# Attention and two feed-forward layers on one core: values with tokens on partitions, the square on another engine, and a new order for the first pass

## The chip, the cores and the metric

The kernel runs on one core of a Trainium2 chip. The metric is the device time of one execution in microseconds (us). Five engines work side by side, each through its own queue of instructions in order: TensorE (PE; its weight loads are listed as PEld), VectorE (DVE), ScalarE (ACT), GpSimd (POOL) and SyncE (SP), which in this kernel does little but issue DMAs.

## What is computed

```python
# attention inside chunks of 64 tokens; q, k, v are (4, 8, 576, 64): batch, heads, tokens, head size
scores = q_c @ k_c.T / 8
attn = softmax(scores)               # maximum taken off; the sum gets 1e-9 added
x = (attn @ v_c) as (2304 tokens, 512)
# layer 1, w_in (512, 2048), w_out (2048, 512)
r = max(x @ w_in, 0);  g = s * (r * r) + b;  x = g @ w_out
# layer 2, the same sizes with weights of its own
h = x @ w_in2;  g = h * tanh(softplus(h));  out = g @ w_out2
```

The weights arrive as 64-bit floats. The kernel reads them as pairs of 32-bit words and decodes each piece into a high and a low part; x and g are split in the same way, and each product is made of three matmuls (high by high, low by high, high by low).

## The kernel before

**Tiles, blocks, chunks.** The 2304 tokens are 18 tiles of 128. Tiles are joined into five blocks of 512, 256, 512, 512 and 512 tokens (`sizes`). The hidden size 2048 is cut into 16 chunks of 128 (d_ff chunks), and four chunks make a group, so each layer has four groups. For a group, each block is multiplied by its four chunks, and the sum of the four is added into `ysum`. The last 7 of 8 groups come from plain loops at the end of the kernel. Attention and the first group of layer 1, the first pass, come from an order written out by hand.

**The order table.** `START` is a string of pieces. `pieces` turns each into instructions, and every engine runs its own in the order of the string. A number is the tile, the weight piece or the step; `@4` names a PSUM bank, and the digit after a dot a buffer. SP has `dk`, `dq`, `dv` (load a tile's keys, queries, values, 256 KB each) and `W` (load a weight piece of 512 KB: 0 to 7 are the first group's, 8 to 15 the second's). PE has `K`, `Q`, `T` (four transposes each of keys, queries, probabilities), `S` (scores), `X` (attention output), `I` and `J` (the two halves of a step's first matmul, `mm_in`), `O` and `P` (the halves of its second, `mm_out`), and `w` followed by a number (that many matmuls on zeros). ACT has the copies out of PSUM `k`, `q`, `t`, the exponential `e`, the high half `x` of a tile's output, the decoding steps `a` and `h`, and `r` (ReLU), `v` (add b) and `g` (high half) of a step. DVE has `m` (row maximum and subtraction), `n` (row sum), `z` (division), `y` (low half), the decoding steps `c`, `d` and `l`, `u` (square times s) and `o` (low half). `E` moves a sum of a block to `ysum`, by turns on ACT and DVE.

A step of a 512-token block is 12 matmuls by the first weights and 12 by the second. A half, `I`, `J`, `O` or `P`, is 6 of them. Before, step i stands for block i // 4 and chunk i % 4.

**Attention of a tile.** Keys and queries are loaded with tokens on partitions, and `K` and `Q` transpose them. `k_out` writes the transposed keys into a block-diagonal buffer `kbd` (two copies of 64 partitions; zeroed by POOL at the start; three of them), so `s_pe` takes 8 matmuls of 128 rows by 64 columns over 128 moving columns. The values are loaded with pairs of heads on partitions, by four DMAs a tile (`load_v`), tile 0's from ACT's queue. `x_pe` takes 16 matmuls of 64 by 64 over 64 columns.

**Buffers that order the loads.** Tiles 0 to 3 keep their keys, queries and values in the room of weight pieces 8 to 15. Later tiles share two buffers for keys, two for queries and three for values, so such a load waits until the `K`, `Q` or `X` that read its buffer is done, and what stands behind it on SP waits too. The sums of a block hold the four PSUM banks `acc0` to `acc3` from its first `O` to its `E`; attention pieces with `@0` to `@3` use the same banks.

Of the kernel before, what the change touches and what calls it, by code (L numbers as in the profile page):

```python
# [9 lines left out]
F32 = mybir.dt.float32  # L10
# [43 lines left out]
def chunk_attention_moe_moe_kernel(  # L54
# [28 lines left out]
    sizes = [512, 256, 512, 512, 512]  # L83
# [120 lines left out]
    def sb_at(i, tag):  # L204

        if i >= NS:
            if tag == "pt":
                return at[i]["e"].rearrange("p h s -> p (h s)")
            return atp.tile([P, DM], F32, tag=tag, bufs=AT_BUFS[tag], name=tag)
        if (i, tag) not in early:  # L210
            if tag in ("e", "pt"):
                whole = sb.tile([P, KD, TB], F32, tag="xhi3" if tag == "e" else "xlo3", name=tag)
                for n in range(NS):
                    early[n, tag] = whole[:, n]
            else:
                both = ("q", "k") if tag in ("q", "k") else ("v", "qt")
                whole = sb.tile([P, 2, DM], F32, tag="w%d_%d" % (tag in ("v", "qt"), NSLOT - 1 - i), name=tag)
                for n, x in enumerate(both):
                    early[i, x] = whole[:, n]
        return early[i, tag]  # L220

    def load_qk(i, which):
        t = sb_at(i, which).rearrange("p (h d) -> p h d", h=H)
        for o, n, bb, ss in runs(i * P, P):
            nc.sync.dma_start(
                out=t[o:o + n],
                in_=(k if which == "k" else q)[bb, :, ss:ss + n, :].rearrange("h s d -> s h d"),
            )
        at.setdefault(i, {})[which] = t

    def load_v(i, eng=nc.sync):
        vn = sb_at(i, "v").rearrange("p (a c d) -> p a c d", a=KD, c=2)
        at.setdefault(i, {})["v"] = vn
        for o, n, bb, ss in runs(i * P, P):
            c0, cn = o // CH, n // CH
            for j in range(2):
                for c in range(cn):
                    eng.dma_start(
                        out=vn[j * CH:(j + 1) * CH, :, c0 + c, :],
                        in_=v[bb, j::2, ss + c * CH:ss + (c + 1) * CH, :].rearrange("a s d -> s a d"),  # L240
                    )
# [7 lines left out]
    def k_pe(i, b):  # L249
        at[i]["kp"] = transposes(b, at[i]["k"].rearrange("p h d -> p (h d)"))  # L250

    def k_out(i, n):
        at[i]["kb"] = kb = kbd[n]
        kp = at[i].pop("kp").rearrange("p a (c s) -> p a c s", c=2)
        for j in range(2):
            sl = slice(j * CH, (j + 1) * CH)
            nc.scalar.copy(out=kb[sl, :, :, sl], in_=kp[sl])  # L257
# [8 lines left out]
    def s_pe(i, b):  # L266
        t = at[i]
        t["sp"] = ps_at(b, [P, H, CH])
        for a in range(KD):
            for c in range(2):  # L270
                sl = slice(c * CH, (c + 1) * CH)
                nc.tensor.matmul(  # L272
                    out=t["sp"][sl, 2 * a:2 * a + 2, :].rearrange("p j s -> p (j s)"),
                    lhsT=t["qt"][:, a, sl],
                    rhs=t["kb"][:, a, c, :],
                )
# [29 lines left out]
    def p_out(i):  # L306
        at[i]["pt"] = sb_at(i, "pt").rearrange("p (a s) -> p a s", a=KD)
        nc.scalar.copy(out=at[i]["pt"], in_=at[i].pop("pp"))

    def x_pe(i, b):  # L310
        t = at[i]
        t["xp"] = ps_at(b, [P, KD, P])
        for a in range(KD):
            for c in range(2):
                for j in range(2):
                    r = slice(j * CH, (j + 1) * CH)
                    s = slice(c * CH, (c + 1) * CH)
                    nc.tensor.matmul(out=t["xp"][r, a, s], lhsT=t["v"][r, a, c, :], rhs=t["pt"][r, a, s])  # L318
# [66 lines left out]
    def mm_out(l, f, g, acc, n, h):  # L385

        w = wt[l, f, 1]
        last = f % FG == FG - 1
# [3 lines left out]
        for p, m in order[h * len(order) // 2:(h + 1) * len(order) // 2]:  # L392
# [6 lines left out]
                start=(f % FG == 0 and p == 0), stop=(last and p == 2),  # L399
# [43 lines left out]

    def pieces(name, i, m, bank):


        b, f = divmod(i, FG)
        n = sizes[b] if b < NB else 0
        if name in ("dk", "dq"):
            load_qk(i, name[1])  # L450
        elif name == "dv":
            load_v(i, nc.sync if i else nc.scalar)
# [5 lines left out]
        elif name == "k":  # L458
            k_out(i, m)
        elif name in "qmenztxy":  # L460
            dict(q=q_out, m=s_max, e=s_exp, n=s_sum, z=s_norm, t=p_out, x=x_hi, y=x_lo)[name](i)
# [13 lines left out]
        elif name == "u":  # L475
            ew_u(ff[i]["r"])
        elif name == "v":
            ew_v(ff[i]["r"])
        elif name == "g":
            ff[i]["g"] = ew_g(ff[i]["r"], n)  # L480
        elif name == "o":
            ff[i]["o"] = ew_o(ff[i]["r"], ff[i]["g"], n)
        elif name in "OP":
            if name == "O" and f == 0:
                first_acc[b] = new_accs(1, b)
            mm_out(1, f, (ff[i]["g"], ff[i]["o"]), first_acc[b], n, "OP".index(name))
        elif name == "E":
            first_sum(i, m, first_acc[i][m], nc.vector.tensor_copy if m % 2 else nc.scalar.copy)
        else:
            raise ValueError(name)  # L490

    with tc.manual_schedule():
# [5 lines left out]
        room = sb.tile([P, 2, KD, 2, P], F32, tag="ysum3", name="kbd12")  # L498
        kbd = [atp.tile([P, KD, 2, P], F32, name="kbd"), room[:, 0], room[:, 1]]
        for kb in kbd:  # L500
            nc.gpsimd.memset(kb, 0.0)
# [8 lines left out]
    def do_out():  # L510
# [3 lines left out]
        for h in range(2):  # L514
            mm_out(l, f, g, accs[l, b], sizes[b], h)
# [55 lines left out]
```

## Time and profile before

| | before |
|---|---|
| median of 3 runs | 889.46 us (888.0 to 890.33) |
| the profiled execution, its own time | 889.39 us |
| its span, first to last instruction | 887.6 us |
| PE busy | 874.8 us, 99% of the span |
| DVE, ACT busy | 477.7 us (54%), 370.9 us (42%) |
| DMA | 53.22 MB, mean 60 GB/s |

The span leaves 1.8 us of the execution's own time outside. A busy share is the share of the span in which the profile shows an instruction of that engine. Matmuls overlap, so the time from one start to the next is what one costs, and not the duration of its row; PE can be listed as busy while it runs slower than it could. The zero matmuls `w` count as busy.

### The profile page before, as it was taken

Reading aid. Unit: us, or ns where it says so; the run is one execution under the profiler, and the core shown is the slowest. Engines: PE = TensorE matmul, PEld = TensorE weight load, DVE = VectorE, ACT = ScalarE, POOL = GpSimd, SP = SyncE. Lnnn points to the kernel's source line nnn. Section 1 sums busy time; section 2 is a strip of 40 time slices with the busy share of each in tenths; the row PEclk is TensorE's granted clock in tenths of the full one; section 3 lists DMA queues with packets and bytes.
Section 4 is the critical chain, followed back from the end, with each engine's and each line's share of the span. In section 5 each row is a group of like instructions: output and inputs, shape, how many; then the busy total and the mean of one; then the engine's idle time right before and its main releaser. Section 6 shows DMA issues by size and latency. Waiting matters only on the chain.

```text
span 887.6 us, 12275 instructions
## 1 busy us (share of the span) xinstructions
PE 874.8 (99%) x4976; PEld 737.9 (83%) x4976; DVE 477.7 (54%) x852; ACT 370.9 (42%) x645; POOL 30.0 (3%) x29
## 2 busy tenths in 40 slices
PE   8989999999999999999999999999999999999997
PEld 7978888888888898888888888888888888888886
DVE  4878875459736943488348922473227722222122
ACT  5667665446534543345445432332223322222221
POOL 1000000000000000002122200000000000000000
PEclk9999999999999999999999999999999999999999
DMA  8996131040004200140004100230003100001012
GB/s 217 220 244 179 44 85 36 21 170 1 1 0 122 69 1 1 48 142 2 1 1 143 48 0 1 61 129 1 0 24 121 46 1 1 0 1 48 24 48 95
DMA packets 81528, 53.22 MB, mean 60 GB/s; under 512 B 58688, under 2 KB 75072, under 8 KB 81472
## 3 DMA queue, kind: packets, MB, share of 16 engines
q1 hardware_dynamic: 80384, 52.18, 20.4%
q8 instruction: 39, 0.64, 0.3%
q10 hardware_dynamic: 1088, 0.26, 0.1%
q14 instruction: 17, 0.14, 0.0%
HBM read 47.71 MB, written 4.72 MB: 59 GB/s over the span
## 4 chain that ended last, share of the span: by engine, by line
PE 97%; ACT 1%; DMA 1%; DVE 0%; issue 0%; DVEq 0%; ACTq 0%
PE hp L344 45%; PE acc L395 45%; PE warm L466 2%; DMA k<-in_k_dram 1%; PE pa L272 1%; ACT kbd L257 1%; PE pa L246 1%; PE pa L318 0%; DVE ysum L416 0%; ACT e L290 0%; ACT v L264 0%; PE pt__383 L272 0%; PE pt__195 L272 0%; PE pt__101 L246 0%; PE pt__2009 L318 0%
## 5 line engine op out<-in xcount | busy, mean ns | idle before, releaser
L344 PE MATMUL hp<-xhi,w 128*128 128x512 f32 (+1 forms) x1280 | 368.6, 369 | 0.3 <-ACT r L354 0.3
L344 PEld LDWEIGHTS hp<-xhi,w 128*128 128x128 f32 x1280 | 232.2, 188 | 41.9 <-issue 0.9
L344 PE MATMUL hp<-xlo,w 128*128 128x512 f32 (+1 forms) x640 | 235.5, 368 | 0.0
L374 DVE TENSOR_TENSOR glo<-r,ghi 128x512 fp32r<-128x512 f32 (+1 forms) x160 | 104.9, 655 | 208.5 <-ACT ghi L369 208.1
L395 PE MATMUL acc<-ghi,w 128*128 128x512 f32 (+1 forms) x640 | 162.8, 372 | 0.0
L395 PE MATMUL acc<-w,ghi 128*128 128x512 f32 x576 | 159.5, 390 | 0.0
L356 ACT ACTIVATE r<-hp 128x512 f32<-128x512 f32 (+1 forms) x80 | 44.4, 555 | 256.5 <-PE hp L344 256.5
L344 PEld LDWEIGHTS hp<-xlo,w 128*128 128x128 f32 x640 | 120.5, 188 | 20.3
L395 PEld LDWEIGHTS acc<-ghi,w 128*128 128x128 f32 x640 | 112.9, 188 | 20.3 <-issue 0.7
L395 PEld LDWEIGHTS acc<-w,ghi 128*128 128x128 f32 x576 | 106.9, 188 | 21.3
L416 DVE TENSOR_TENSOR ysum<-acc,ysum 128x512 f32<-128x512 f32 (+1 forms) x114 | 71.8, 656 | 58.7 <-PE acc L395 58.7
L369 ACT ACTIVATE ghi<-r 128x512 fp32r<-128x512 f32 (+1 forms) x160 | 94.0, 588 | 7.5 <-PE acc L395 3.6
L395 PE MATMUL acc<-w,glo 128*128 128x512 f32 x288 | 93.9, 389 | 0.0
L395 PE MATMUL acc<-glo,w 128*128 128x512 f32 (+1 forms) x320 | 92.9, 369 | 0.0
L360 DVE SCALAR_TENSOR_TENSOR r<-r,s_sb 128x512 f32<-128x512 f32 (+1 forms) x80 | 56.3, 704 | 56.6 <-ACT r L354 56.4
L354 ACT ACTIVATE r<-hp 128x512 f32<-128x512 f32 (+1 forms) x80 | 44.3, 554 | 97.1 <-PE hp L344 96.2
L365 ACT ACTIVATE r<-r,b_sb 128x512 f32<-128x512 f32 (+1 forms) x80 | 54.2, 679 | 44.8 <-DVE r L360 44.6
L395 PEld LDWEIGHTS acc<-glo,w 128*128 128x128 f32 x320 | 58.1, 188 | 10.2
L395 PEld LDWEIGHTS acc<-w,glo 128*128 128x128 f32 x288 | 54.1, 188 | 11.3
L173 ACT ACTIVATE w<-wdec 128x512 fp32r<-128x512 f32 x64 | 40.1, 628 | 23.3 <-DVE wdec L164 22.7
L178 DVE TENSOR_TENSOR w<-wdec,w 128x512 fp32r<-128x512 f32 x64 | 44.8, 702 | 2.8 <-ACT w L173 2.2
L160 DVE SCALAR_TENSOR_TENSOR wdec<-wraw,wdec 128x512 uint32<-128x512 uint32 x64 | 43.9, 691 | 0.4
(249 smaller groups left out, 506.4 us busy)
## 6 DMA issues: line engine op xcount, KB each, us to landing
wraw<-in_moe_w_in_dram SPq DMA_DIRECT2D x32, 512.0 KB, 4.0
wraw<-in_moe_w_out_dram SPq DMA_DIRECT2D x32, 512.0 KB, 3.6
out_dram<-ysum SPq DMA_DIRECT2D x18, 256.0 KB, 2.0
v<-in_v_dram SPq DMA_DIRECT2D x68, 64.0 KB, 2.9
k<-in_k_dram SPq DMA_DIRECT2D x16, 256.0 KB, 4.3
q<-in_q_dram SPq DMA_DIRECT2D x12, 256.0 KB, 4.9
k<-in_q_dram SPq DMA_DIRECT2D x4, 256.0 KB, 4.7
k<-in_k_dram SPq DMA_DIRECT2D x4, 128.0 KB, 4.3
```

Source lines behind the costliest of these rows:

```text
L160: nc.vector.scalar_tensor_tensor(out=u, in0=t[:, :, 1], scalar=0xC0000000, in1=u, op0=ALU.bitwise_and, op1=ALU.bitwise_or,)
L173: nc.scalar.activation(out=w[:, 0], in_=a, func=AF.Copy)
L178: nc.vector.tensor_tensor(out=lo, in0=a, in1=hi.bitcast(F32), op=ALU.subtract)
L344: nc.tensor.matmul(out=hp, lhsT=w[:, sl], rhs=r[b][:, a, :], start=(a == 0 and p == 0), stop=(a == KD - 1 and p == 2),)
L354: nc.scalar.activation(out=r, in_=hp, func=AF.Relu)
L356: nc.scalar.activation(out=r, in_=hp, func=AF.Mish)
L360: nc.vector.scalar_tensor_tensor(out=r, in0=r, scalar=s_sb[:, 0:1], in1=r, op0=ALU.mult, op1=ALU.mult)
L365: nc.scalar.activation(out=r, in_=r, func=AF.Identity, bias=b_sb[:, 0:1])
L369: nc.scalar.activation(out=hi, in_=r, func=AF.Copy)
L374: nc.vector.tensor_tensor(out=lo, in0=r, in1=hi.bitcast(F32), op=ALU.subtract)
L395: nc.tensor.matmul(out=acc[m][:, :n] if l == 1 else acc[m], lhsT=w[wi][:, sl] if l == 1 else g[gi][:, sl], rhs=g[gi] if l == 1 else w[wi], ...
L416: nc.vector.tensor_tensor(out=y, in0=a[:, :w], in1=y, op=ALU.add)
```

## The change

- **Values.** One helper `load` serves keys, queries and values: values too get tokens on partitions and one DMA for a tile (two where a tile spans two batches), all from SP.
- **Which side is block-diagonal.** `k_out` is one copy of 128 partitions into one of four plain buffers `kt`, and `s_pe` takes 16 matmuls of 64 by 64 over 64 columns. `p_out` writes the transposed probabilities into one of three block-diagonal buffers `pbd` with two copies of 64 partitions, and `x_pe` takes 8 matmuls of 128 by 64 over 128 columns.
- **The square.** In the first pass `u` is a Square on ACT, and `v`, also on ACT, multiplies by s and adds b. The later groups keep the square on DVE.
- **Blocks and segments.** The blocks are 512, 512, 256, 512 and 512 tokens. In the first pass blocks 0 and 1 take turns over the chunks, as `SEGMENTS` says: block 0 chunk 0, block 1 chunks 0 and 1, block 0 chunks 1 to 3, block 1 chunks 2 and 3, then blocks 2, 3 and 4. Step i is the i-th of that list. A block's second segment is added to `ysum` by four additions on DVE, so there are 28 pieces `E` in place of 20.
- **The order.** `START` is written anew. It holds 17 matmuls on zeros in place of 76.

```diff
+SEGMENTS = (
+    (0, (0,)),
+    (1, (0, 1)),
+    (0, (1, 2, 3)),
+    (1, (2, 3)),
+    (2, (0, 1, 2, 3)),
+    (3, (0, 1, 2, 3)),
+    (4, (0, 1, 2, 3)),
 )
...
-    sizes = [512, 256, 512, 512, 512]
+    sizes = [512, 512, 256, 512, 512]
...
+    def load(i, which):
+        at.setdefault(i, {})[which] = t = sb_at(i, which)
         for o, n, bb, ss in runs(i * P, P):
             nc.sync.dma_start(
+                out=t[o:o + n].rearrange("p (h d) -> p h d", h=H),
+                in_=dict(k=k, q=q, v=v)[which][bb, :, ss:ss + n, :].rearrange("h s d -> s h d"),
             )
...
     def k_out(i, n):
+        at[i]["kt"] = kt[n]
+        nc.scalar.copy(out=kt[n], in_=at[i].pop("kp"))
...
+                for j in range(2):
+                    r = slice(j * CH, (j + 1) * CH)
+                    s = slice(c * CH, (c + 1) * CH)
+                    nc.tensor.matmul(out=t["sp"][r, 2 * a + c, :], lhsT=t["qt"][r, a, s], rhs=t["kt"][r, a, s])
...
+    def p_out(i, n):
+        at[i]["pb"] = pb = pbd[n]
+        pp = at[i].pop("pp").rearrange("p a (j s) -> p a j s", j=2)
+        for c in range(2):
+            sl = slice(c * CH, (c + 1) * CH)
+            nc.scalar.copy(out=pb[sl, :, :, sl], in_=pp[sl])
...
+                nc.tensor.matmul(
+                    out=t["xp"][r, a, :], lhsT=t["v"][:, h * CH:(h + 1) * CH], rhs=t["pb"][:, a, j, :]
+                )
...
         elif name == "u":
-            ew_u(ff[i]["r"])
+            nc.scalar.activation(out=ff[i]["r"], in_=ff[i]["r"], func=AF.Square)
         elif name == "v":
-            ew_v(ff[i]["r"])
+            nc.scalar.activation(
+                out=ff[i]["r"], in_=ff[i]["r"], func=AF.Identity, scale=s_sb[:, 0:1], bias=b_sb[:, 0:1]
+            )
...
         elif name == "E":
-            first_sum(i, m, first_acc[i][m], nc.vector.tensor_copy if m % 2 else nc.scalar.copy)
+            eb = SEGMENTS[i][0]
+            if eb in [z[0] for z in SEGMENTS[:i]]:
+                w = sizes[eb]
+                y = ysum[eb][:, m * w:(m + 1) * w]
+                nc.vector.tensor_tensor(out=y, in0=first_acc[i][m][:, :w], in1=y, op=ALU.add)
+            else:
+                first_sum(eb, m, first_acc[i][m], nc.vector.tensor_copy if m % 2 else nc.scalar.copy)
```

The new table: PE's first 69 pieces, SP's first 56, and ACT's from the first ReLU to the first `E` (banks and buffers left out):

```
PE: K0 Q0 Q7 S0 Q4 K7 K4 S7 Q2 S4 Q1 K1 K3 T0 K5 S1 K6 K2 X0 T7 S2 Q3 Q5 X7 T4 S5 S3 T1 K9 X4 Q6 X1 K13 S6 T2 w14 X2
    Q9 T3 T5 S9 X3 T6 X5 w3 K12 X6 Q13 I0 Q12 J0 S13 K15 I1 K10 J1 S12 I2 I3 Q11 J3 Q8 J2 I4 O0 K17 P0 J4 K8 ...
SP: dk0 dq0 dq7 dq4 dv0 dk7 dk4 dq1 dq2 sb dk1 dk3 dv4 dk5 dk6 dk2 dv2 dv7 dq3 dq5 dv1 W1 W0 dk9 dq6 dv3 dk13 dv5
    W5 W7 W2 dq9 W6 dv10 W3 W4 dk12 dv6 dq13 dk15 dq12 dv13 dk10 W14 W13 W15 W8 dq8 dq11 W11 dv8 W12 W10 dk17 W9 dk8 ...
ACT: ... r0 h1 u0 k15 v0 e9 g0 k10 e13 a2 r1 h3 u1 v1 a7 g1 q11 h2 r3 q8 u3 a4 v3 e12 r2 g3 E0.0 ...
```

## Rows read from the trace of the kernel before

**Rows 1.** The page: PE's busy time, and the chain that ended last by line.
```profile
PE 874.8 (99%) x4976; PEld 737.9 (83%) x4976; DVE 477.7 (54%) x852; ACT 370.9 (42%) x645; POOL 30.0 (3%) x29
...
PE hp L344 45%; PE acc L395 45%; PE warm L466 2%; DMA k<-in_k_dram 1%; PE pa L272 1%; ACT kbd L257 1%; PE pa L246 1%; PE pa L318 0%; DVE ysum L416 0%; ACT e L290 0%; ACT v L264 0%; PE pt__383 L272 0%; PE pt__195 L272 0%; PE pt__101 L246 0%; PE pt__2009 L318 0%
```

**Rows 2.** Windows: PE, PEld, DVE, ACT, POOL busy; granted clock, DMA share, GB/s.
```profile
0.00:55.00 55.00, 46.95 (x558) 43.57 (x560) 35.21 (x70) 33.98 (x59) 3.38 (x9) 1.00 0.90 220
...
55.00:75.00 20.00, 19.71 (x177) 16.07 (x175) 16.97 (x30) 15.01 (x28) 0.00 (x0) 1.00 0.97 280
74.40:193.60 119.20, 119.19 (x988) 99.04 (x989) 77.87 (x143) 67.71 (x121) 0.00 (x0) 1.00 0.28 74
193.60:293.60 100.00, 100.00 (x487) 84.59 (x486) 71.49 (x132) 52.92 (x93) 0.00 (x0) 1.00 0.13 40
...
40.00:50.00 10.00, 8.48 (x126) 7.69 (x125) 8.22 (x18) 5.92 (x11) 0.00 (x0) 1.00 0.78 191
```

**Rows 3.** Timeline of PE, first 56 us: start, duration, instruction [idle before].
```profile
3.89 1.09 PE L246 MATMUL pt__101<-ident,k 128*128 128x128 f32 x4 [3.89 <-DMA k<-in_k_dram]
4.77 1.49 PE L466 MATMUL warm<-zero 128*128 128x128 f32 x6
...
12.08 0.83 PE L466 MATMUL warm<-zero 128*128 128x128 f32 x6
12.75 0.60 PE L246 MATMUL pa<-ident,k 128*128 128x128 f32 x4
13.18 0.83 PE L466 MATMUL warm<-zero 128*128 128x128 f32 x6
...
18.07 1.09 PE L272 MATMUL pa<-kbd,qt 128*64 128x128 f32 x16
19.10 1.15 PE L318 MATMUL pa<-pt,v 64*64 64x64 f32 x32
20.18 0.66 PE L246 MATMUL pt__277<-ident,k 128*128 128x128 f32 x4
...
53.79 0.65 PE L246 MATMUL pa<-ident,k 128*128 128x128 f32 x4 [0.72 <-DMA k<-in_k_dram]
...
55.89 0.72 PE L344 MATMUL hp<-xhi,w 128*128 128x512 f32 x2
```

**Rows 4.** Timeline of PE, 74 to 194 us.
```profile
74.41 0.50 PE L344 MATMUL hp<-xhi,w 128*128 128x256 f32 x2 [0.29 <-ACT r L354]
...
104.91 0.88 PE L395 MATMUL acc<-ghi,w 128*128 128x256 f32 x6
105.62 0.63 PE L344 MATMUL hp<-xhi,w 128*128 128x512 f32 x2
...
185.47 1.98 PE L395 MATMUL acc<-ghi,w 128*128 128x512 f32 x8
...
188.19 1.98 PE L395 MATMUL acc<-ghi,w 128*128 128x512 f32 x8
...
193.63 0.62 PE L344 MATMUL hp<-xhi,w 128*128 128x512 f32 x2
```

**Rows 5.** Timeline of SP's DMA issues.
```profile
40.72 2.76 SPq L238 DMA_DIRECT2D v<-in_v_dram  x4
...
46.90 0.55 SPq L225 DMA_DIRECT2D k<-in_k_dram  x1
```

**Rows 6.** Groups by line and shape, 0 to 220 us: busy us, mean ns | idle before.
```profile
L360 DVE SCALAR_TENSOR_TENSOR r<-r,s_sb 128x512 f32<-128x512 f32 x20 | 14.9, 744 | 7.9 <-ACT r L354 7.9
L365 ACT ACTIVATE r<-r,b_sb 128x512 f32<-128x512 f32 x20 | 14.4, 718 | 2.6 <-DVE r L360 2.5
...
L369 ACT ACTIVATE ghi<-r 128x512 fp32r<-128x512 f32 x20 | 12.6, 629 | 0.8 <-PE acc L395 0.6
...
L257 ACT COPY kbd<-pa 64x512 f32<-64x512 f32 x18 | 10.4, 581 | 10.6 <-PE pa L246 10.4
...
L493 ACT ACT_TABLE_LOAD x1 | 1.3, 1283 | 0.7 <-PEq L555 0.7
```

More of the change, by code (lines that the diff above doesn't have):

```diff
@@ L206, in sb_at @@
         if i >= NS:
-            if tag == "pt":
-                return at[i]["e"].rearrange("p h s -> p (h s)")
             return atp.tile([P, DM], F32, tag=tag, bufs=AT_BUFS[tag], name=tag)
         if (i, tag) not in early:
-            if tag in ("e", "pt"):
-                whole = sb.tile([P, KD, TB], F32, tag="xhi3" if tag == "e" else "xlo3", name=tag)
+            if tag == "e":
+                whole = sb.tile([P, KD, TB], F32, tag="xhi3", name=tag)
                 for n in range(NS):
@@ L220, in sb_at @@
         return early[i, tag]
-    def load_qk(i, which):
-        t = sb_at(i, which).rearrange("p (h d) -> p h d", h=H)
+    def load(i, which):
+        at.setdefault(i, {})[which] = t = sb_at(i, which)
         for o, n, bb, ss in runs(i * P, P):
             nc.sync.dma_start(
-                out=t[o:o + n],
-                in_=(k if which == "k" else q)[bb, :, ss:ss + n, :].rearrange("h s d -> s h d"),
-            )
[L229 to L241, printed above, removed]
+                out=t[o:o + n].rearrange("p (h d) -> p h d", h=H),
+                in_=dict(k=k, q=q, v=v)[which][bb, :, ss:ss + n, :].rearrange("h s d -> s h d"),
+            )
     def transposes(b, src):
@@ L249, in k_pe @@
     def k_pe(i, b):
-        at[i]["kp"] = transposes(b, at[i]["k"].rearrange("p h d -> p (h d)"))
+        at[i]["kp"] = transposes(b, at[i]["k"])
     def k_out(i, n):
[L253 to L257, printed above, removed]
+        at[i]["kt"] = kt[n]
+        nc.scalar.copy(out=kt[n], in_=at[i].pop("kp"))
     def q_pe(i, b):
-        at[i]["qp"] = transposes(b, at[i]["q"].rearrange("p h d -> p (h d)"))
+        at[i]["qp"] = transposes(b, at[i]["q"])
     def q_out(i):
@@ L270, in s_pe @@
             for c in range(2):
[L271 to L276, printed above, removed]
+                for j in range(2):
+                    r = slice(j * CH, (j + 1) * CH)
+                    s = slice(c * CH, (c + 1) * CH)
+                    nc.tensor.matmul(out=t["sp"][r, 2 * a + c, :], lhsT=t["qt"][r, a, s], rhs=t["kt"][r, a, s])
     def s_max(i):
@@ L304, in p_pe @@
         at[i]["pp"] = transposes(b, at[i]["e"].rearrange("p h s -> p (h s)"))
-    def p_out(i):
-        at[i]["pt"] = sb_at(i, "pt").rearrange("p (a s) -> p a s", a=KD)
-        nc.scalar.copy(out=at[i]["pt"], in_=at[i].pop("pp"))
+    def p_out(i, n):
[4 more added lines that the diff above has]
+            nc.scalar.copy(out=pb[sl, :, :, sl], in_=pp[sl])
     def x_pe(i, b):
@@ L313, in x_pe @@
         for a in range(KD):
[L314 to L318, printed above, removed]
+            for j in range(2):
+                r = slice(j * CH, (j + 1) * CH)
+                h = 2 * a + j
+                nc.tensor.matmul(
+                    out=t["xp"][r, a, :], lhsT=t["v"][:, h * CH:(h + 1) * CH], rhs=t["pb"][:, a, j, :]
+                )
     def x_hi(i):
@@ L383, in ew, with mm_out @@
         return hi, ew_o(r, hi, n)
-    def mm_out(l, f, g, acc, n, h):
+    def mm_out(l, f, g, acc, n, h, first, last):
         w = wt[l, f, 1]
-        last = f % FG == FG - 1
         order = [(p, m) for p in range(3) for m in range(len(acc))]
@@ L398, in mm_out @@
                 rhs=g[gi] if l == 1 else w[wi],
-                start=(f % FG == 0 and p == 0), stop=(last and p == 2),
+                start=(first and p == 0), stop=(last and p == 2),
             )
@@ L442, in new_accs @@
         ]
+    steps = [
+        (b, f, e, o == 0, o == len(fs) - 1) for e, (b, fs) in enumerate(SEGMENTS) for o, f in enumerate(fs)
+    ]
     def pieces(name, i, m, bank):
[L447 to L452, printed above, removed]
+        b, f, e, begins, ends = steps[i] if i < len(steps) else (0, 0, 0, False, False)
+        n = sizes[b]
+        if name in ("dk", "dq", "dv"):
+            load(i, name[1])
         elif name == "sb":
@@ L457, in pieces @@
             dict(K=k_pe, Q=q_pe, S=s_pe, T=p_pe, X=x_pe)[name](i, bank)
[L458 to L461, printed above, removed]
+        elif name in "kt":
+            dict(k=k_out, t=p_out)[name](i, m)
+        elif name in "qmenzxy":
+            dict(q=q_out, m=s_max, e=s_exp, n=s_sum, z=s_norm, x=x_hi, y=x_lo)[name](i)
         elif name in "Wacdhl":
@@ L475, in pieces @@
         elif name == "u":
-            ew_u(ff[i]["r"])
+            nc.scalar.activation(out=ff[i]["r"], in_=ff[i]["r"], func=AF.Square)
         elif name == "v":
-            ew_v(ff[i]["r"])
+            nc.scalar.activation(
+                out=ff[i]["r"], in_=ff[i]["r"], func=AF.Identity, scale=s_sb[:, 0:1], bias=b_sb[:, 0:1]
+            )
         elif name == "g":
@@ L483, in pieces @@
         elif name in "OP":
-            if name == "O" and f == 0:
-                first_acc[b] = new_accs(1, b)
-            mm_out(1, f, (ff[i]["g"], ff[i]["o"]), first_acc[b], n, "OP".index(name))
+            if name == "O" and begins:
+                first_acc[e] = new_accs(1, b)
+            mm_out(1, f, (ff[i]["g"], ff[i]["o"]), first_acc[e], n, "OP".index(name), begins, ends)
         elif name == "E":
-            first_sum(i, m, first_acc[i][m], nc.vector.tensor_copy if m % 2 else nc.scalar.copy)
+            eb = SEGMENTS[i][0]
[5 more added lines that the diff above has]
+                first_sum(eb, m, first_acc[i][m], nc.vector.tensor_copy if m % 2 else nc.scalar.copy)
         else:
@@ L497, in chunk_attention_moe_moe_kernel @@
         warm = ps_h.tile([P, TB], F32, tag="h", name="warm")
[L498 to L501, printed above, removed]
+        room = sb.tile([P, 2, KD, 2, P], F32, tag="ysum3", name="pbd12")
+        pbd = [atp.tile([P, KD, 2, P], F32, name="pbd"), room[:, 0], room[:, 1]]
+        kt = sb.tile([P, 4, KD, P], F32, tag="ysum4", name="kt")
+        kt = [kt[:, n] for n in range(4)]
+        for pb in pbd:
+            nc.gpsimd.memset(pb, 0.0)
         for w in START.split():
@@ L514, in do_out @@
         for h in range(2):
-            mm_out(l, f, g, accs[l, b], sizes[b], h)
+            mm_out(l, f, g, accs[l, b], sizes[b], h, f % FG == 0, f % FG == FG - 1)
         if f % FG == FG - 1:
```

45 rows, old and new, of the table START are left out of this document.

## The prediction

> **What bounds the kernel now.** I read the page first. PE is busy for 99% of the span, and the chain that ended last runs through its two feed-forward lines, 45% and 45%; zero matmuls have 2% of it and loads of keys 1% [rows 1]. A busy share includes zeros and slow matmuls, so I went on to the windows by stage [rows 2]. They show two kinds of time. Up to 75 us the DMAs are the full resource: their share is 0.90 up to 55 us and 0.97 from there to 75. Afterwards it is 0.28 and less, and PE has no gap. The timeline of PE says where the border is: a transpose of keys still waits for its load at 53.79, the first feed-forward matmul starts at 55.89 [rows 3], and the last gap, 0.29 us, ends at 74.41 [rows 4]. From there PE sets the pace to the end. The first pass ends at 193.63, where the second group starts [rows 4].
>
> The waste follows from prices taken start to start. Four transposes cost 0.43 us (12.75 to 13.18), S 1.03 (18.07 to 19.10), X 1.08 (19.10 to 20.18), a zero matmul 0.22 (six rows, three matmuls, in 0.67 us) [rows 3]. A half of a 512-token step costs 1.36 (twelve matmuls from 185.47 to 188.19) and of a 256-token step 0.71 (104.91 to 105.62) [rows 4]. The first pass is 54 sets of transposes, 18 S, 18 X, 64 large and 16 small halves: 23.2 + 18.5 + 19.4 + 87.0 + 11.4 = 159.6 us. It takes 193.6. Of the 34 us between, 3.9 pass before the first load is there [rows 3] and 17 go to 76 zero matmuls; the rest is waits and changes between kinds of matmul. All this lies in the stage that the loads set. A new order can win there and nowhere else: from 193.6 on the work is the same, with the 256-token block third and not second, and PE has no gap that its place could open or close. I cost that move at 0.
>
> **The change, part by part.** *S and X trade shapes.* The new S is the old X's 16 matmuls of 64 by 64, the new X the old S's 8, so a tile costs PE 1.08 + 1.03 as before: 0. *The copies trade too:* two 64-partition copies of 0.58 us [rows 6] move from keys to probabilities: 0 for ACT. POOL's zeroing leaves the path of the first keys.
>
> *Square.* DVE loses 0.74 us a step. No row shows a Square. Below it is bounded by no loss, were it hidden, and above by the dearest ACT row, 0.72 with b as an operand; I take 0.63, the high-half copy [rows 6]. Twenty squares put about 12 us on ACT, which has 67.7 of 119.2 us busy after 74.4 [rows 2]. There the cost is 0; PE covers it. In the stage before it could show (a rival, below). *The eight sums* that DVE now adds are some 0.7 us each, less than the 14 us of squares that leave DVE; between the last P of a segment and the next O stand at least 2 us of other PE pieces. I take 0.
>
> *The loads of values.* SP spends 2.76 us on the four DMAs of a tile's values and 0.55 on a load of keys [rows 5]. A tile's values are as many bytes as its keys. Between 40 and 50 us, when SP issues two tiles' values, the DMAs' share falls to 0.78 [rows 2]. One DMA in place of four frees about 2.2 us of SP for a tile, and the share can rise toward 1. What is behind on SP gains: all later loads.
>
> *The order, and its sum.* In the new table PE meets the loads at few places. Up to Q13 it has 28 sets of transposes, 9 S, 8 X and 17 zeros, 33.7 us of work, and must wait for the load dq13, behind 30 tile loads and 8 weight pieces: 12.06 MB. Then it is I0's turn. The next places are Q11, and K17, whose load stands behind 38 tile loads and 15 weight pieces: 38 x 0.262 + 15 x 0.524 = 17.83 MB. K8 needs 0.79 MB more, 2.8 us at 280 GB/s, which P0 and J4 (2.7) and K17's transposes cover. After that PE has more work than loads.
>
> When does dk17 land? Before, 12.1 MB moved up to 55 us and 5.6 from there to 75, 17.7 MB in all [rows 2]. At that pace, shared idle time and all, 17.83 MB are in at 75.5. With no idle time the same bytes are 0.90 x 55 + 0.97 x 20 = 68.9 us of sixteen engines, so 69.4 for ours, and about 2.9 us pass before (the first load of 0.26 MB, 1 us at that pace, is used at 3.89 [rows 3]): 72.3. I take 73.6, nearer the second, since values by single DMAs take away the one cause of idle DMAs that the rows show; both ends are kept. The waits of SP for buffers I cost at 0: each K, Q or X for which a load up to dk17 must wait stands in PE's order at least 3 us before SP needs it.
>
> What is left at K17? I compare it with the gapless stretch from 74.41 to 193.63, 119.2 us [rows 4], so that the changes between kinds are priced in. That held 56 large halves, 14 small ones, 22 sets of transposes, 8 S and 11 X. After K17's wait there are 54, 16, 20, and 7 S and 10 X in their new shapes: 2 x 1.36 + 2 x 0.43 + 4 x 1.08 less, 2 x 0.71 + 2 x 1.03 more, 4.4 us less in all. So 114.8 remain, and the pass ends at 73.6 + 114.8 = 188.4, **5.2 us earlier**. The profiled execution took 889.4 (span 887.6 and 1.8 around it), which is the median of the runs within 0.1 us: **884.2 us**, 0.6% faster.
>
> The same sum from Q13 checks it. dq13 is in at 52.3 without idle DMAs (12.06 MB at 220 / 0.90 = 244 GB/s are 49.4 us, and 2.9 before) and at 54.8 at the old 220 GB/s. From 55.89 on the old pass took 137.7 us; what is queued from Q13 is three 64-by-64 sets less, 134.5. That gives 186.8 to 189.3 if nothing waits later. The gain is small although 59 zero matmuls go, because they stood in waits: the loads, not the zeros, held PE.
>
> **The rivals.** *The loads come in no denser, or ACT holds the stage back: no change.* At the old pace K17 waits until 75.5: 190.3, so 886.1. ACT then has 27 instructions between r0 and E0.0, about 17 us at 0.63 [rows 6], in the 17 to 18 us from J0's end to K17. If it falls 3 us behind, O1 waits for E0.2 as long: 193.3, 889.1. For it: ACT has 15.0 of 20 us busy there without squares [rows 2]. Against: its rows overlap by some 0.1 us, and the exponentials, copies and highs of later tiles aren't needed at once.
>
> *The clock stays low: slower.* The granted clock reads 1.00 of 2.4 GHz in all windows [rows 2], but the six zero rows at 4.77 take 1.49 us and those at 12.08 0.83 [rows 3]: the start ran at the 1.2 GHz level, and twelve zero matmuls around Q3 came ahead of the rise. The new table has no zeros until w14, and two thirds of its pieces up to there are transposes. If the low level lasts to w14's end, 23 sets, 8 S and 4 X cost 2 x 22.7 = 45.3, with 3.9 and 6.2 for w14 55.4, and 8.4 more to I0: 63.8. With 134.1 from there the pass ends at 197.9, 4.3 later: 893.7. It decides at about 30 us: up to there the lost work, 13 us of 26, is made good in the waits for loads before I0, and each us after costs half of one. Against: at the low level the pieces cost twice as much, so PE has hardly a gap, which is what came ahead of the rise before.
> The Trainium skill, "TensorE: Matmul & The Clock Gate", Part 4, says that the full clock does not engage for transposes, which don't count as PE work in the same way. By that rule this rival would hold; by the rows above, where zeros and transposes stand mixed ahead of the rise, neither is shown. The granted clock and the length of the early transposes after the change will tell.
>
> *Square needs a table of its own: slower.* One table load is 1.28 us [rows 6]. Two for each square would add 2.6 us to twenty steps, 51 us to ACT: with 68 + 12 it exceeds the 115 us that PE leaves, and in the full stage three squares cost 8 us at once: 188.4 + 8 or more, 892 and up. Only one load is in the rows, for a pass that mixes six functions.
> The Trainium skill, "ScalarE: Activation LUTs", section "Table sets", says that cheap functions are filler in every set; it names relu, copy, identity and abs, not square.
>
> **How the numbers follow.** The forecast (K17's load sets the end; 187.1 to 190.3, so 882.9 to 886.1, and 880 if weight pieces come in at the better rate of the second window) has a chance of 0.68. Loads no denser with ACT behind, 886 to 890: 0.17. Low clock, 888 to 894: 0.11. Tables: 0.04. The range from 880 to 890 leaves out the upper part of the low clock and the tables, and a little below. Runs of this kernel spread by 0.3%, 2.7 us, so 0.3% is what can be told from no change. Below 886.8 lies the forecast with a part of the second case, 0.68; within 2.7 us the rest of that and half of the low clock, 0.20; above 892.1 0.12.
>
> **What would show it.** Right: DMAs' share above 0.95 up to 70 us; I0 starting at 52 to 55; short waits for DMAs at Q11 and K17; no PE gap after about 74; the second group at 187 to 190, and the same 694 us after it. Wrong: early transposes of 0.9 us (clock); PE waiting for ACT or DVE between 55 and 90; more than one table load in the first pass; SP waiting for K, Q or X before 70 us.

## The result, and the profile after

The changed kernel took **880.84 us** (median of 4 runs, 879.42 to 882.30); the kernel before, run beside it on the same chip, 889.89 (4 runs, 888.00 to 890.91). The ratio is 0.9896, with a 95% interval from 0.9878 to 0.9914: **1.0% faster**. Forecast were 884.2 us, 0.6% faster, and a range of 880 to 890. The side is right, the time lies inside the range near its lower end, and the gain is 1.7 times the forecast one.

The page first: PE's busy line, and the chain that ended last, by engine and by line. Against [rows 1] PE is busy 10 us less, 118 of its rows are gone (59 zero matmuls, two rows each), and the zero matmuls (PE warm) have left the chain; transfers now have 4% of it.

```profile
PE 864.7 (98%) x4858; PEld 725.5 (82%) x4858; DVE 469.8 (53%) x840; ACT 383.9 (44%) x665; POOL 30.0 (3%) x29
...
PE 93%; DMA 4%; SPq 2%; DVE 0%; issue 0%; DVEq 0%
PE acc L392 45%; PE hp L342 44%; DMA q<-in_q_dram 2%; SPq L235 1%; DMA k<-in_k_dram 1%; DMA v<-in_v_dram 1%; PE pa L269 0%; PE pa L243 0%; SPq L143 0%; PE pa L314 0%; DVE ysum L413 0%; SPq L453 0%; PE pt__1332 L269 0%; PE pt__1747 L269 0%; PE pt__1632 L269 0%
```

Windows of the changed kernel, columns as in [rows 2]; the first two answer to the first two there, and the last two stretches are the gapless rest of the first pass and the loops behind it.

```profile
0.00:55.00 55.00, 44.43 (x579) 37.21 (x580) 35.08 (x70) 34.39 (x60) 3.38 (x9) 0.97 0.96 241
55.00:75.00 20.00, 18.91 (x145) 14.91 (x145) 14.01 (x27) 16.91 (x32) 0.00 (x0) 1.00 0.97 288
12.00:14.00 2.00, 2.00 (x47) 1.65 (x44) 1.90 (x6) 0.80 (x2) 0.00 (x0) 1.00 0.51 109
20.00:22.00 2.00, 2.00 (x33) 1.78 (x32) 0.00 (x0) 1.68 (x4) 0.00 (x0) 0.50 1.00 226
...
74.40:186.90 112.50, 112.50 (x875) 94.09 (x874) 72.40 (x134) 77.58 (x136) 0.00 (x0) 1.00 0.25 66
186.90:286.90 100.00, 100.00 (x487) 84.66 (x487) 72.05 (x133) 53.69 (x93) 0.00 (x0) 1.00 0.12 40
```

In the first 55 us the loads run at 241 GB/s where they ran at 220. From 74.4 us PE has no gap, as before.

The timeline of PE has the three places that decide: the first step (line 342 for the first time), the transposes of K17 with their wait, and the start of the second group.

```profile
51.01 1.09 PE L314 MATMUL pa<-pbd,v 128*64 128x128 f32 x16 [1.38 <-DMA v<-in_v_dram]
52.03 0.65 PE L243 MATMUL pt__710<-ident,q 128*128 128x128 f32 x4
52.44 0.71 PE L342 MATMUL hp<-xhi,w 128*128 128x512 f32 x2
...
65.40 0.66 PE L243 MATMUL pa<-ident,q 128*128 128x128 f32 x4 [0.60 <-DMA q<-in_q_dram]
...
72.49 0.66 PE L243 MATMUL pt__955<-ident,k 128*128 128x128 f32 x4 [0.49 <-DMA k<-in_k_dram]
...
186.94 0.62 PE L342 MATMUL hp<-xhi,w 128*128 128x512 f32 x2
```

The first step comes 3.45 us earlier than the 55.89 of [rows 3], the second group 6.69 earlier than the 193.63 of [rows 4], and from there to the end it is 880.5 - 186.94 = 693.6 us, where it was 887.6 - 193.6 = 694.0. So 6.7 of the 7.1 us that the spans differ by lie ahead of the second group. The four executions took 879.42, 879.58, 882.09 and 882.3 us, so the median stands between two pairs and is the time of none. The profiled one is the 882.3; another of the same kernel (the first experiment) took 879.9, and the difference is there too, in the first pass.

### The profile page after: what moved, and what is told of

The parts are those of the page before. It is cut to its first block, busy times and chain, and to the rows that moved or that the text cites. A ratio compares the mean times of both kernels' runs of the same rounds, so it can differ in the third digit from the quotient of the medians.

```text
span 880.5 us, 11971 instructions
## 1 busy us (share of the span) xinstructions
PE 864.7 (98%) x4858; PEld 725.5 (82%) x4858; DVE 469.8 (53%) x840; ACT 383.9 (44%) x665; POOL 30.0 (3%) x29
## 3 DMA queue, kind: packets, MB, share of 16 engines
q1 hardware_dynamic: 80640, 52.44, 20.4%
## 4 chain that ended last, share of the span: by engine, by line
PE 93%; DMA 4%; SPq 2%; DVE 0%; issue 0%; DVEq 0%
PE acc L392 45%; PE hp L342 44%; DMA q<-in_q_dram 2%; SPq L235 1%; DMA k<-in_k_dram 1%; DMA v<-in_v_dram 1%; PE pa L269 0%; PE pa L243 0%; SPq L143 0%; PE pa L314 0%; DVE ysum L413 0%; SPq L453 0%; PE pt__1332 L269 0%; PE pt__1747 L269 0%; PE pt__1632 L269 0%
## 5 line engine op out<-in xcount | busy, mean ns | idle before, releaser
L358 DVE SCALAR_TENSOR_TENSOR r<-r,s_sb 128x512 f32<-128x512 f32 (+1 forms) x60 | 42.5, 709 | 48.8 <-ACT r L352 48.8
L363 ACT ACTIVATE r<-r,b_sb 128x512 f32<-128x512 f32 (+1 forms) x60 | 40.9, 682 | 42.3 <-DVE r L358 42.2
```

Source lines behind the costliest of these rows:

```text
L358: nc.vector.scalar_tensor_tensor(out=r, in0=r, scalar=s_sb[:, 0:1], in1=r, op0=ALU.mult, op1=ALU.mult)
L363: nc.scalar.activation(out=r, in_=r, func=AF.Identity, bias=b_sb[:, 0:1])
```

## The experiments

All times are medians beside runs of the kernel before on the same chip (889.4, 890.9, 890.6 and 891.1 us in four sessions), the ratio is against these. *First step*, *K17* and *group 2* are starts on the timeline of PE; share and GB/s are of the window from 0 to 55 us. These columns are of the one profiled execution, which need not be the median one: e3's took 883.54 us and e9's 881.49. K17 is left out where the old order stands, which has it late.

| kernel | us | ratio, 95% interval | share, GB/s | first step | K17 | group 2 |
|---|---|---|---|---|---|---|
| before | 889.9 | 1 | 0.90, 220 | 55.89 | | 193.63 |
| changed | 880.84 | 0.9896 [0.9878, 0.9914] | 0.96, 241 | 52.44 | 72.49 | 186.94 |
| e1 changed, again | 879.98 | 0.9894 [0.9874, 0.9913] | 0.99, 250 | 50.86 | 70.02 | 184.47 |
| e2 zeros early | 883.67 | 0.9929 [0.9912, 0.9947] | 0.94, 235 | 53.46 | 73.75 | 188.18 |
| e3 no zeros | 880.40 | 0.9898 [0.9879, 0.9918] | 0.94, 236 | 53.26 | 73.78 | 188.19 |
| e4 square on DVE | 880.33 | 0.9893 [0.9874, 0.9912] | 0.98, 246 | 50.99 | 70.22 | 184.66 |
| e5 values by four | 890.68 | 0.9996 [0.9987, 1.0005] | 0.84, 215 | 58.93 | 80.72 | 195.58 |
| e6 old order | 886.36 | 0.9944 [0.9931, 0.9956] | 0.97, 238 | 53.12 | | 190.84 |
| e7 before, no zeros | 891.05 | 0.9996 [0.9987, 1.0005] | 0.88, 214 | 57.75 | | 195.49 |
| e8 weights late | 882.47 | 0.9897 [0.9880, 0.9913] | 0.94, 236 | 54.28 | 73.17 | 187.53 |
| e9 constants late | 883.32 | 0.9918 [0.9901, 0.9935] | 0.98, 249 | 50.11 | 71.69 | 186.10 |
| e10 values by two | 885.09 | 0.9938 [0.9922, 0.9954] | 0.91, 230 | 55.69 | 76.16 | 190.57 |
| e11 old order, no zeros | 886.46 | 0.9950 [0.9934, 0.9966] | 0.95, 230 | 53.28 | | 190.94 |
| e12 constants on ACT | 882.05 | 0.9902 [0.9886, 0.9918] | 0.94, 237 | 52.85 | 72.23 | 186.66 |

**The clock: e1, e2, e3.** e1 is the changed kernel unaltered.

> The changed kernel once more, unaltered, for more executions and a second trace. Its four times so far are 879.4, 879.6, 882.1 and 882.3 us, and the trace of the 882.3 shows a granted clock of 0.83 and 0.50 between 18 and 22 us. Clock theory: the two pairs are executions without and with that dip; a trace at about 879.5 shows 1.00 from 10 us on and the first pass ending near 184.2, one at 882.2 shows a dip and 186.9. Rival (loads alone): the dip costs nothing because the loads set the pace there; both kinds of trace show the same first pass, and the 2.7 us lie elsewhere, after 187 us.

e2 puts zero matmuls ahead of two waits, e3 takes all of the new table's 17 out.

```diff
- ... q2 dv7 Q1@1 ... k1.3 K5@5 W1 ...
+ ... q2 dv7 w2 Q1@1 ... k1.3 w6 K5@5 W1 ...
```

> The changed kernel with two zero matmuls ahead of Q1 and six ahead of K5, in the waits at 15 and 17 us. Clock theory: no dip near 20 us, all executions near 879.5, so a median 0.1 to 0.2 percent under that of the unaltered one. Loads alone: no difference. Zeros as a burden: 8 x 0.22 = 1.8 us later at the most.

> The changed kernel without its 17 zero matmuls, which stand in waits for loads before Q9 and K12. Clock theory: gaps of 4 to 5 us near 38 us let the clock fall, the pieces from Q9 on start at half pace, and the first feed-forward step comes 1 to 3 us later: 881 to 884. Loads alone: the wait only changes its name, 880.8, no difference.

The rows at the start of the changed kernel answer the low-clock rival. Timeline of PE, first 24 us:

```profile
3.95 1.09 PE L243 MATMUL pt__99<-ident,k 128*128 128x128 f32 x4 [3.95 <-DMA k<-in_k_dram]
...
7.11 1.98 PE L269 MATMUL pa<-kt,v 64*64 64x64 f32 x32
9.02 0.66 PE L243 MATMUL pa<-ident,q 128*128 128x128 f32 x4
...
19.16 1.02 PE L243 MATMUL pt__266<-ident,k 128*128 128x128 f32 x4 [1.88 <-DMA k<-in_k_dram]
20.11 1.97 PE L269 MATMUL pa<-kt,qt 64*64 64x64 f32 x32
22.02 0.98 PE L243 MATMUL pa<-ident,k 128*128 128x128 f32 x4
22.83 0.60 PE L243 MATMUL pa<-ident,q 128*128 128x128 f32 x4
```

Four transposes take 1.09 us at first and 0.66 from 9.02 on: after three sets of transposes and one S, without a zero matmul, PE runs at full pace. Then PE waits 1.88 us for K5's keys, and K5, S1 and K6 run at half pace: granted clock 0.50 from 20 to 22 us, the 1.2 GHz level. From K5's start to K2's the three take 3.67 us. e1 waits 1.75 us at the same place, the clock stays at 1.00, and they take 2.15:

```profile
19.41 0.66 PE L243 MATMUL pt__266<-ident,k 128*128 128x128 f32 x4 [1.75 <-DMA k<-in_k_dram]
19.99 1.15 PE L269 MATMUL pa<-kt,qt 64*64 64x64 f32 x32
21.07 0.66 PE L243 MATMUL pa<-ident,k 128*128 128x128 f32 x4
21.56 0.60 PE L243 MATMUL pa<-ident,q 128*128 128x128 f32 x4
```

So a fall of the clock comes in some executions and costs PE 1.5 us here. Part of that goes into later waits: X2 starts 0.68 us later than in e1 (41.00 against 40.32). Over the executions a fall isn't what makes the two pairs of times: in e1 those with the lowest mean clocks, 0.997 and 0.998, took 880.11 and 879.53 us, and one at 0.999 took 881.38. So my clock theory, which the two traces fit, does not hold for the rest.

The zeros are no cure: e2 is 3.7 us slower than e1, its neighbour on the same chip, which is more than the 1.8 us that eight zeros are worth. In its profile the clock falls later (0.50 from 28 to 30 us, behind a wait of 2.07 us for queries). But its other five executions had a mean clock of 1.000 and took 881.45 to 885.37 us, so the clock isn't what makes e2 slow. Up to 24.8 us its trace runs as e1's does; then two weight pieces issued at 23.44 kept SP 3.50 us, where e1 needed 1.53, and queries came late. Why is open. e3 is the same as changed within the interval.

The Trainium skill, "TensorE: Matmul & The Clock Gate", Part 4, says that the full clock does not engage for transposes. Here one S, 16 small matmuls (32 rows), stands among 12 transposes ahead of the rise, so no run shows what transposes alone do.

**Square back to DVE: e4.** Both operations of the chunk as before, everything else new.

```diff
- nc.scalar.activation(out=ff[i]["r"], in_=ff[i]["r"], func=AF.Square)
+ ew_u(ff[i]["r"])
- nc.scalar.activation(... func=AF.Identity, scale=s_sb[:, 0:1], bias=b_sb[:, 0:1])
+ ew_v(ff[i]["r"])
```

> The changed kernel with the first pass's square back on DVE (times s there, then b on ACT), in the same places of the order. My forecast costs the move at 0, so no difference: within 1 us of 880.8, and ACT some 12 us less busy before 187 us. Rival: the move is part of the gain, since DVE and ACT must keep up between 55 and 90 us; then PE waits for DVE there and the time is 882 or more.

880.33: no difference, as forecast. The window from 55 to 75 us of e4 and then of e1, each from its own trace, shows the work change sides (DVE third, ACT fourth) while PE's stays:

```profile
55.00:75.00 20.00, 19.55 (x143) 15.97 (x138) 18.42 (x34) 16.02 (x30) 0.00 (x0) 1.00 1.02 298
```

```profile
55.00:75.00 20.00, 19.61 (x138) 15.99 (x135) 16.29 (x30) 18.32 (x33) 0.00 (x0) 1.00 1.01 290
```

In the changed kernel's groups by line and shape from 55 to 187 us the sixteen squares of 512 tokens are line 475, at 0.63 us, as taken. With s as a second operand `v`, line 477, costs 0.81, where the old one cost 0.72 [rows 6]. DVE's eight sums are line 493, at 0.67:

```profile
L477 ACT ACTIVATE r<-r,b_sb,s_sb 128x512 f32<-128x512 f32 x16 | 13.0, 814 | 0.3
L475 ACT ACTIVATE r<-r 128x512 f32<-128x512 f32 x16 | 10.1, 632 | 0.3
```

```profile
L493 DVE TENSOR_TENSOR ysum<-acc,ysum 128x512 f32<-128x512 f32 x8 | 5.2, 672 | 0.8 <-PE acc L392 0.8
```

The first pass has one table load of 1.28 us, as before: Square needs none of its own.

**How many transfers carry the values: e5, e10.** The new order and layouts, but each tile's values by four DMAs of 64 KB, and by two of 128 KB.

```diff
-            nc.sync.dma_start(out=t[o:o + n]..., in_=...[bb, :, ss:ss + n, :]...)
+            for c in range(cuts):      # 4 in e5, 2 in e10, of values alone
+                nc.sync.dma_start(out=t[o:o + n, c-th heads]..., in_=...[bb, c-th heads, ss:ss + n, :]...)
```

> The changed kernel with each tile's values loaded by four DMAs (two heads each, all tokens) in place of one; bytes, packet size, layout and order are unaltered. My forecast: SP's issues and the DMAs outstanding limit the loads again; the DMAs' share up to 55 us falls from 0.96 to about 0.90, K17 waits until 75 to 76, and the time is 3 us more, 883 to 885. Rival: the share is set by the waits for buffers and not by the number of DMAs; no difference, 880 to 882.

> The new kernel with each tile's values brought by two DMAs of 128 KB in place of one of 256 (four gave the whole gain back). Theory, that the number of loads that SP can issue and have outstanding sets the rate at which bytes come: two cost about a third of what four cost, 883 to 885, with the DMAs' share between 0.84 and 0.96 up to 55 us. Rival, that only the issue time of SP matters: a tile's values by two DMAs cost SP some 1.1 us, still less than the bytes take (1 us at 250 GB/s), so nothing is lost, 880 to 882, share 0.95 or more.

Four give back the whole gain, 1.0% and not the 3 us that my forecast gave; two give back 0.4%, some 4 us, which my theory for e10 had forecast (883 to 885, share 0.91). That does not settle it against its rival: by the rival's own numbers two issues take 1.1 us and the bytes 1 us, so it should have forecast a loss too. Windows and timeline of SP's issues in e5:

```profile
0.00:55.00 55.00, 41.84 (x542) 34.74 (x542) 29.35 (x60) 31.29 (x55) 3.38 (x9) 0.94 0.84 215
55.00:75.00 20.00, 16.68 (x148) 13.09 (x149) 14.36 (x25) 13.48 (x25) 0.00 (x0) 1.00 0.91 240
...
10.00:30.00 20.00, 15.47 (x197) 12.85 (x196) 10.46 (x21) 10.97 (x20) 0.00 (x0) 0.83 0.79 175
```

```profile
19.64 5.06 SPq L238 DMA_DIRECT2D v<-in_v_dram  x8
24.74 0.47 SPq L238 DMA_DIRECT2D k<-in_q_dram  x1
```

The eight DMAs of two tiles' values keep SP 5.06 us for 0.52 MB, about 104 GB/s, and everything behind them on its queue waits. In the trace each of SP's loads waits for the one eight before it, so at most eight can be outstanding. But these eight places are not what holds the loads. In the changed kernel SP issues 65 loads in 72 us, one every 1.1 us, and a load of 256 KB lands 3.8 to 4.7 us (medians) after its issue starts, a weight piece 6.5 to 7.3, so four to five are outstanding. The load eight before had landed 1.2 us or more before each issue up to 72 us, in e10 0.8; in e5 two issues start within 0.1 us of it. With four DMAs a tile about five are outstanding (87 loads in 72 us, landing after 3.1 to 6.2 us), and a quarter of the size then means fewer bytes under way. Whether SP's time for an issue (0.4 us at the least, for 64 KB as for 256) or this small number sets the rate, no run separates. The clock falls in both profiles (0.66 from 20 to 30 us). In e5 PE still waits 1.33 us for keys at 56.25, just ahead of the first step, so the loads set it. In e10 PE has no wait after 39.85 us, and X6 starts at 54.25, 1.0 us after its values landed; that much of e10's loss may be the low clock from 40 to 44 us (0.62 and 0.52).

The old order suffers less from the same four DMAs (0.97 and 245 GB/s from 10 to 30 us of the kernel before, 0.79 and 175 here): there 512 KB weight pieces stand between the values of single tiles [rows 5], here values of two tiles come together and only one pair of weight pieces before 30 us. That reading is from the rows; no run tried the spacing by itself.

**The order by itself: e6, e7, e11.** e6 has the new layouts and single-DMA values with the old table, blocks, segments and Square on DVE; e11 is e6 without the table's 76 zero matmuls, e7 the kernel before without them.

```diff
- "dk0 dq0 dq7 dq4 dv0 K0@4 dk7 k0.0 ...       sizes = [512, 512, 256, 512, 512]
+ "dk3 dq3 dv0 dv3 K3@4 dk2 dq2 k3.0 w3 ...    sizes = [512, 256, 512, 512, 512]
- ... k3.0 w3 Q3@5 dk4 q3 dq4 w9 S3@0 ...      (e7, e11: every w taken out)
+ ... k3.0 Q3@5 dk4 q3 dq4 S3@0 ...
```

> The new layouts (values with tokens on partitions by one DMA, plain keys, block-diagonal probabilities) with the old order table, the old blocks and the square on DVE. Order theory: denser loads bring the load of K10 some 3 us forward, and the first step with it, 3 to 4 us in all: 886 to 887, so the larger part of the 9 us comes from the new order. Rival (layout): the layouts alone give most of it, 882 or less. Rival (order alone): no difference to the kernel before, 889 to 890.

> The kernel before without its 76 zero matmuls. My forecast says that they stood in waits, so nothing is won, 889 to 890, or lost through a low clock in the first 50 us, up to 893. Rival: the zeros held PE up, and taking 17 us of them away is most of the gain: 880 to 884.

> The new layouts with the old order and blocks (which gave 886.4), without its 76 zero matmuls of some 17 us. In the kernel before, taking them out gave nothing, since they stood in waits for loads. Theory: here the loads come denser, so PE runs with fewer waits and the zeros have become real work: the time falls to 881 to 883, and most of what the new order is worth is that it drops zeros. Rival: the loads are still what PE meets last before the first step, so nothing changes (885.5 to 887) and the worth of the new order lies in where it meets the loads.

By the ratios the layouts with single DMAs give 0.56%, and the new order on top of them the other 0.48%; by e5 the new order and layouts without the single DMAs give nothing. (No run has the single DMAs in the old layout, so those two aren't told apart.) Taking the 76 zeros out changed nothing beyond the intervals, about 0.1% in e7 and 0.2% in e11, so my theory for e11, that denser loads had made work of them, fell. Where they stood PE now waits for loads. PE's longest waits in e7, by what was waited for (us in total, times, longest; the last is the first load, as before):

```profile
PE pa L246 <- DMA k<-in_k_dram: 5.8, 3, 3.4
PE pt__298 L246 <- DMA k<-in_k_dram: 5.6, 1, 5.6
PE pt__101 L246 <- DMA k<-in_k_dram: 3.9, 1, 3.9
```

What the order brings is seen in the table above. The first step comes 0.7 and 2.3 us earlier (53.12 in e6, 52.44 and 50.86 in changed and e1), and what is queued behind it takes PE 137.7 us in the old order (190.84 - 53.12; 193.63 - 55.89 before) and 134.5 or 133.6 in the new.

**K17's load: e8.** Eight weight pieces that nothing needs soon are issued behind the loads that PE waits for.

```diff
- l0 W14 y5 ... W13 I0 ... W15 q13 c3 W8 ... dq11 W11 S13@5 ... W12 I1 u0 W10 k15.2 dk17 m13 ... W9 e9 J1 dk8 g0
+ l0 y5 ... I0 ... q13 c3 ... dq11 W14 S13@5 ... I1 u0 k15.2 dk17 W13 m13 ... e9 J1 dk8 W15 W8 W11 W12 W10 W9 g0
```

> The changed kernel with the loads of the second group's eight weight pieces moved behind dq11, dk17 and dk8 on SP. My forecast says K17's load sets the end; then its wait (0.5 us) and Q11's (0.6) go, and as Q13's load, 8 us of work ahead, is the next limit, 1.1 us are won: about 879.7. Rival: the later weight pieces (needed by ACT from about 80 us on) come too late, ACT and with it PE stalls, and the time is 881 or more.

The waits at Q11 and K17 are gone, and the time is the same: 0.9897 against 0.9896. The intervals, 1.5 us to either side, are wider than the 1.1 us that I forecast, so the times can't tell; the traces can. From the first step to group 2 this profile has 187.53 - 54.28 = 133.25 us, with no wait in it. That stretch is 134.5 in changed and 133.6 in e1, so the waits cost 0.4 to 1.25 us there. But the step starts at 54.28, later than in changed and e1, though on SP nothing ahead of Q13's load was moved. X6 and Q13 take 2.67 us here, at a granted clock of 0.50 from 52 to 54 us, and 1.43 in changed:

```profile
51.61 1.98 PE L314 MATMUL pa<-pbd,v 128*64 128x128 f32 x16 [0.78 <-DMA v<-in_v_dram]
53.52 1.12 PE L243 MATMUL pt__708<-ident,q 128*128 128x128 f32 x4
54.28 0.99 PE L342 MATMUL hp<-xhi,w 128*128 128x512 f32 x2
```

The other 0.6 us is X6's wait for its values, which ends at 51.61 and not at 51.01. So this execution was late for reasons that its edit did not touch.

**The two small constants: e9, e12.** From 12 to 14 us the changed kernel's DMAs are busy 0.51 (above), right behind two loads of 0.5 KB. SP's rows for these two last from 9.01 to 10.77 us, 1.8 us of its queue for 1 KB. They take two of the eight places as well, but no issue near them waits for a place. e9 moves them behind W14, e12 to ACT's queue ahead of everything.

```diff
- ... dq2 sb dk1 ...
+ ... dq2 dk1 ... l0 W14 sb y5 ...                  (e9)
+ nc.scalar.dma_start(out=s_sb, ...); nc.scalar.dma_start(out=b_sb, ...)   before the table, no sb in it (e12)
```

> The new kernel with the load of its two small constants (0.5 KB each) moved from the first 10 us to behind the fourth-pass weight load W14, some 40 us later. In the trace of the new kernel the DMAs' share falls to 0.51 in the two us behind these loads, and the waits of SP's issues show that every load waits for the one eight before it: two tiny loads take two of eight places. If outstanding loads set the pace of the start (the theory), about 1 us of sixteen engines is won: the 12 to 14 us window at 0.9 or more and a time 0.5 to 1 us below the unaltered new kernel, 879 to 880. If the start is set by PE's own pieces or by the bytes alone (the rival), 880 to 882 as before.

> The new kernel with its two constants loaded by ACT's queue before anything else, in place of SP's at 9 to 11 us. Moved to 51 us on SP's queue, they let the DMAs' share from 12 to 14 us rise from 0.51 to 1.08 and brought the first step to 50.1 us, but the sum with the constant then waited 2.4 us for them on ACT, PE 1.1 us for ACT, and the keys of K17 came late. Theory: with them in at the start, the first gain stays and the later wait goes: the 12 to 14 us window near 1, first step at 50 to 51.5 us, remaining 133.6 to 134.5 us, so 878.5 to 880.5, 0.5 to 1 us below the unaltered new kernel's runs. Rival: one us won at the start is lost again at Q11 or K17, where the bytes set the time: 880 to 882, no difference.

In e9 the dent is gone (1.08 from 12 to 14 us) and the first step is the earliest of all, 50.11 (in the fastest of its five executions). Then ACT waits 2.4 us for the constant that it adds to the first chunk, PE waits for ACT, and SP, which waits for PE to free buffers, issues K17's keys late:

```profile
62.32 0.72 PE L342 MATMUL hp<-xhi,w 128*128 128x512 f32 x2 [1.12 <-ACT r L352]
...
71.69 0.66 PE L243 MATMUL pt__955<-ident,k 128*128 128x128 f32 x4 [0.94 <-DMA k<-in_k_dram]
...
186.10 0.61 PE L342 MATMUL hp<-xhi,w 128*128 128x512 f32 x2
```

In e12 the dent is gone as well (1.12), but the first keys come 0.5 us later (PE starts at 4.46), and the first step isn't earlier. In neither is anything won, as the rivals had it, though half a us would not show in these intervals; e9 with the later wait is even some 2 us slower, at the edge of them. No version here is faster than the changed kernel.

## Why the prediction was right, and where its size was off

*The stage and the bound* were right. From 74.4 us on there is no gap, and from group 2 to the end it is 693.5 to 693.9 us in every trace of the new layouts, against 694.0: the block of 256 in another place is worth nothing, as costed.

*The edits at nothing* were right: Square by e4, the zeros by e3, e7 and e11, the sums by the gapless stretch. PE never waits for ACT or DVE behind the first step: its two waits there, 0.60 and 0.49 us, are for loads. ACT has 77.6 us of work from 74.4 to 186.9, where 67.7 + 12 was expected of it.

*What remains at K17* was right to 0.35 us. Forecast were 114.8; measured are 186.94 - 72.49 = 114.45, and between 114.36 and 114.86 in the nine other traces of the new order, while K17 itself moves from 70.0 to 80.7 us. So the time of each of them can be told from one row: K17's start, 114.4, some 693.7, and 1.8 around the span.

*When dk17 lands* is the term that was mis-sized. The prediction took 73.6, between 72.3 and 75.5. PE had its keys at 72.49 in the one trace of the changed kernel and at 70.02 in the other, below the lower bound; medians of 880.84 and 879.98 stand for about 71 and 70. The lower bound capped the loads at the old rate with idle time taken out, 220 / 0.90 = 244 GB/s up to 55 us. They ran at 241 and 250, with shares of 0.96 and 0.99, so a full share carried 251 to 253. The prediction also shied away from its own lower end, for idle time that was not there. That the median lies inside the range is partly luck: e1, the same kernel, came out at 879.98, just below it. Of the 3.4 us between forecast and median, 1.1 is this term in the profiled execution (73.6 to 72.49), 0.35 the rest of the pass (114.8 to 114.45) and 0.4 the loops behind it; the last 1.5 are that the profiled execution is the slowest of four; the faster ones, by the sum above, met K17 near e1's 70.02.

*The step "K17's load sets the end"* was right of the row, and too much of the cause. With K17's and Q11's waits gone (e8) only 0.4 to 1.25 us of the stretch go. What decides is the first step, the prediction's second sum: it moves from 50.11 to 58.93 us over the traces of the new order, while the stretch behind it stays between 133.25 and 136.65. The wait that this sum named was one load off. PE meets the values of tile 6 (X6, the row at 51.01 above) before it comes to Q13, and Q13 then has no wait. In changed, e1, e2, e4, e9 and e12 the first step starts 1.43 or 1.44 us after X6. Both loads stand next to each other on SP, so the sum came out near: Q13's queries landed at 51.5 us in changed and 50.0 in e1, where 52.3 to 54.8 was forecast (12.06 MB at a full share's 251 GB/s and 2.9 us would be 50.9). That sum gave 186.8 to 189.3 for the second group, and its "134.5 if nothing waits" is 133.25 when nothing does.

*SP's waits for buffers* were said not to be there, and before 70 us were named as a sign of being wrong; they are there. In the changed kernel SP waits 14 us up to 72 us for PE to be done with a buffer (before: 3.5). The longest, by what was waited for, up to 72 us:

```profile
SPq L235 <- PE pa L243: 5.1, 5, 2.4
SPq L235 <- PE pt__811 L243: 3.5, 1, 3.5
SPq L235 <- PE acc L392: 2.5, 1, 2.5
```

On the whole they came to little: e1 has as much, 14.5 us, at a share of 0.99 up to 55 us and 1.01 from there to 75, and in changed the share from 55 to 75 is 0.97. But it falls to 0.51 from 62 to 64 us, behind the wait of 3.5. They do tie the late loads to PE: what delays PE before 65 us delays K17's keys, as e9 shows.

*The single DMAs* were priced as 2.2 us of SP for a tile, a share toward 1, and no more. The share came (0.96 and 0.99 up to 55 us, forecast above 0.95 up to 70; from 60 to 70 us changed has 0.89). What the prediction did not see is that the new order needs them: it took the loads "no denser" to mean 886, and with four DMAs for a tile in the new order they came less dense than before, 215 GB/s, and the time was 890.7. The rival "loads no denser" named the mechanism and priced it at 886.1, too little.

*The low clock* happened, but in pieces: 1.5 us in one profiled execution, nothing in another, and the times don't follow it. *The tables* did not.

## What to carry to other kernels

Where a stage waits for loads, count the transfers as well as the bytes: with four to five loads outstanding, small or large, values in four pieces a tile cost 1.0%, in two 0.4%, and an order written for single loads was worth nothing without them. Find the one place after which nothing waits, and check that what is left from there is constant over variants (114.4 here): then a variant's time can be told from one row, and a wait that remains can be priced by taking it away. Filler matmuls that stood in waits for loads were free in three kernels, and so was taking them out; eight put into such waits went with 3.7 us more (e2), so measure them.

## What the runs showed that was not expected

- A wait of 1.88 us was followed by three pieces at the 1.2 GHz level (3.67 us) in one execution, and one of 1.75 us at the same place by none in another; with zeros put ahead of that wait five of six executions kept a mean clock of 1.000, and took 3.7 us more.
- Two loads of 0.5 KB leave the sixteen DMA engines half idle for 2 us (0.51), and removing that dent in two ways won nothing that shows.
- In one kernel's two profiles the first step differs by 1.6 us and the time by 2.4: the stage of the loads makes the spread between executions.
